# Windowed attention and a split-precision FFN on one core: probabilities moved for two chunks at once, ring loads taken from ScalarE's queue, runs of attention two pairs apart

## The chip, the cores and the metric

The kernel runs on one core of one Trainium2 chip. The metric is the device time of one execution in microseconds. The kernel before took 993.02 us (median of 3 runs, 989.14 to 995.45).

## The reference

```
# q, k, v: (8 batches, 8 heads, 576 tokens, 64), float32
scores = (q @ k^T) / 8;  masked to rel = pos_q - pos_k in [0, 64), else -1e9
p      = exp(scores - rowmax);  p = p / (sum(p) + 1e-9)
x      = (p @ v) laid out as (4608 tokens, 512)
h      = x @ w_in            # 512 -> 2048
g      = h * tanh(softplus(h))
out    = g @ w_out           # 2048 -> 512, float32
```

All of it is float32. The matrix products of the FFN are made of three products of rounded parts (high by high, high by low, low by high).

## The kernel before

**Plain chunks.** The 4608 tokens are 12 chunks of 384. Chunks 0 to 3 are computed in 64 steps n (16 per chunk): a step makes `h_ps` from x and one 128-column slice of `wi` (w_in, resident on chip), ScalarE applies Mish, and the step's `gh`, `gl` go through `wo_h`, `wo_l` into three accumulators `acc`.

**Wides.** The other eight chunks are computed as four "wides" of two chunks. A wide runs through NG=8 "pairs" g, each of two slices of w_in, and a pair is made of seven products (A11, S2, A12, S3, S1, A22, S4, a Strassen-Winograd scheme) in banks `m_ps`, with `u` and `t` as the sums between them. The weights' sums for the seven products are made once (`make_sums`), stored to DRAM in `sums` and streamed back into a ring of two pairs that takes the place of part of `wi` (`load_sums`, called by `next_load` for pair g+2 as soon as the products of pair g have read a piece). The activations' sums are put into other places of `wi` (`SLOTS`) by the `fills`, before the first pair of a wide.

**Attention of a wide.** While a wide is computed, `Wide.run(k)` makes the attention of the next one, a pair of heads k at a time, for both of its chunks ("halves" u). A run first makes the value products of heads k-1 (`at<-pT,v_t`, 24 matmuls per half), then the score products of heads k (`s_ps`). Then DVE masks the scores and finds their maxima, ScalarE takes the exponentials, DVE normalizes (`normal`) and transposes in 32 by 32 blocks into `tr`, and DMAs on SP's queue (`load`, which is `nc.sync`) move the blocks from `tr` to their partitions in `pT` (`each_move`). The value products of a half wait for all moves of that half. `RUNS` says after which pair of the wide before a run stands: `RUNS = {0: 0, 1: 1, 3: 2, 5: 3, 6: 4}`, so run 1 follows one pair after run 0, and run 4 one pair after run 3. The runs of the first wide stand in the last plain steps, at n = 45, 49, 53, 57 and 61 (`first_runs`).

**Shared tiles.** `st0`, `st1` and `st2` are three places of one buffer each. The `tr` of the halves, `w`, `s` and `two` of `make_sums`, and `u` of the wides lie in them in turn, and each new tenant waits until the reads of the last one are over.

**Order.** PE executes in the order in which the code is written. Of the other engines each has its own queue, and its order is set by a scheduler; a queue is worked off strictly in order, and a waiting instruction holds up what is behind it. DMAs take one of eight completion counters in turn (DMAHW0 to DMAHW7 in the rows), and a DMA waits until the one that had its counter before has landed.

Of the kernel before, what the change touches and what calls it, by code (L numbers as in the profile page):

```python
# [10 lines left out]
F32 = mybir.dt.float32  # L11
# [13 lines left out]
TQ = 32  # L25
# [4 lines left out]
def tile_window_attn_mish_ffn(  # L30
# [81 lines left out]
            for k in range(0, TK, TQ):  # L112
                engine.tensor_copy(all_masks[r:r + TQ, :, k:k + TQ], all_masks[r:r + TQ, :, k + TQ:k + 2 * TQ])

    pTs = [const.tile([P, P // 32, HM, 32], F32, name=f"pT{i}") for i in range(2)]
    vec.memset(ident, 0.0)
    masks_built = build_masks(pool, vec)
    both_pT = pTs
    pTs = itertools.cycle(pTs)

    wi = const.tile([P, NF, 2, NC_, P], F32R, name="wi")
# [29 lines left out]
    def at_set(n, name):  # L151
        return ps_at.tile([P, DO], F32, name=name, tag=f"at{n}")
# [615 lines left out]
    atts[3].plan(begin, (starts[3] - ahead - begin) / (NPAIR + 0.5), lag=1.5)  # L768
    begin = starts[3] - ahead

    sums = tc.dram_tile([NG, NPROD, P, 2 * 2 * P], F32, name="sums")
    flat = wi.rearrange("p f l c n -> p (f l c n)")
    RING = NPROD * 2 * 2 * P
    ring = flat[:, :2 * RING].rearrange("p (g m n) -> p g m n", g=2, m=NPROD)
    XS = 2 * 2 * CH
    LOADS = ((0, 2), (2, 4), (4, 6), (6, 7))

    def make_sums(g):

        f0, f1 = 2 * g, 2 * g + 1  # L780
        for m, f, half in ((A11, f0, 0), (A12, f0, 1), (A22, f1, 1)):
            nc.sync.dma_start(sums[g, m].rearrange("p (l n) -> p l n", l=2),
                              wi[:, f, :, 2 * half:2 * half + 2, :].rearrange("p l c n -> p l (c n)").bitcast(F32))
        w = st_home([P, 2, 2, 2 * P], F32, "w", 0)
        parts = [wi[:, f0:f1 + 1, i, :, :].rearrange("p f c n -> p f (c n)").bitcast(F32) for i in range(2)]
        nc.vector.tensor_tensor(w.rearrange("p f h n -> p f (h n)"), *parts, ALU.add)
# [5 lines left out]
        for n, ms in ((2, (S2, S3)), (0, (S1, S4))):  # L792
# [7 lines left out]
    def load_sums(g, first, end):  # L800
# [12 lines left out]
    class Wide:  # L813
# [16 lines left out]
        def run(self, k):  # L830

            at = [at_set(i, "at") for i in range(2)]
            if k >= 1:
                for u, a in enumerate(self.atts):
                    value_products(a.v[k - 1], a.pT.pop(k - 1), [at[u][:, n:n + BLK] for n in range(0, CH, BLK)])
            if k < NPAIR:
                banks = [h_bank("s_ps", DO) for _ in range(2)]
                s_ps = {}
                for u, a in enumerate(self.atts):
                    for m in range(NM):  # L840
                        n = u * NM + m
                        to = [(banks[h], n * TK) if n < 5 else (at[h], CH) for h in range(2)]
                        to = [b[:, i:i + TK] for b, i in to]
                        thin_products(a.qk[k], m, to)
# [12 lines left out]
            units = [new_probs(TK) for _ in range(2)]  # L857
            todo = [(u, h, m) for h in range(2) for u in range(2) for m in range(NM) if (u, m) != (1, NM - 1)]
            todo += [(1, h, NM - 1) for h in range(2)]
            for u, h, m in todo:  # L860
                s = [[None] * NM for _ in range(2)]
                s[h][m] = s_ps[u, h, m]
                done = masked(self.cs[u], units[u], s, [(h, m)])
                if copies and (u, m) == (1, NM - 1):
                    tc.add_manual_dep(done.ins, copies[h].ins.name, SYNC, reason="one reader of a bank at a time")
            for u, a in enumerate(self.atts):
                normal(units[u], BY_HEAD)
                pT, each = run_transpose(units[u][0], both_pT[u], u)
                a.pT[k] = pT, list(each)
                self.after(u, k, "qk")  # L870

        def after(self, u, k, what):
# [31 lines left out]
            yield self.fill(S4, b22)  # L904

        def product(self, g, m, bank, start):
            w = ring[:, g % 2, m, :].rearrange("p (l k n) -> p l k n", l=2, k=2)
# [19 lines left out]
        def pair(self, g, some, between):  # L927
            def bank():
                return h_bank("m_ps")

            def t_tile():
                return mp.tile([P, CH], F32, name="t", tag="t", bufs=TS)

            def add(out_, a, b):
                with tc.high_priority(offset=SOON):
                    nc.vector.tensor_tensor(out_, a, b, ALU.add)  # L936

            u2, u3 = (kept["u"][:, i, :] for i in range(2))
# [7 lines left out]
            self.next_load(g, 0)  # L946
# [6 lines left out]
            self.next_load(g, 1)  # L953
            add(u3, u2, b)
            some(2)
            a = bank()
            self.product(g, S1, a, True)
            t = t_tile()
# [3 lines left out]
            self.next_load(g, 2)  # L962
# [5 lines left out]
            self.next_load(g, 3)  # L968
            t = t_tile()
            add(t, u2, a)  # L970
            units[0, 1] = self.unit(None, t)
            some(2)
            between(g)
            some(NG * NTT)
            return units

        def next_load(self, g, n):
            if g + 2 < NG or self.next:
                load_sums(g + 2, *LOADS[n])
# [87 lines left out]
    for n, (c, f) in enumerate(steps):  # L1067
# [117 lines left out]
```

## Time and profile before

| | |
|---|---|
| median of 3 runs | 993.02 us (989.14 to 995.45) |
| the profiled execution | 991.94 us, span 990.1 us |
| mean granted clock of TensorE in it | 0.952 of full |
| PE busy | 894.3 us, 90% of the span |
| ScalarE (ACT) busy | 459.8 us, 46% |
| VectorE (DVE) busy | 435.0 us, 44% |
| GpSimd (POOL) busy | 240.5 us, 24% |
| queue of DMAs by hardware, q1 | 143.05 MB, 45.4% of 16 engines' time |
| moves of probabilities | 480 of 24 KB, 1.8 us from issue to landing |
| ring loads | 96 of 512 KB and 32 of 256 KB, about 4 us to landing |

Busy time is per engine. PE is busy for nine tenths of the span, so what can be read from the rest is where PE stood still and what released it. The granted clock is the share of full speed (2.4 GHz) that the throttle gave TensorE; 0.5 is its lower level of 1.2 GHz.

### The profile page before, as it was taken

How to read it: one execution, taken by the hardware profiler on the slowest of the kernel's cores; microseconds unless marked ns; L12 is line 12 of the kernel's file. 1: busy time of each engine (PE TensorE's matmuls, PEld its weight loads, DVE VectorE, ACT ScalarE, POOL GpSimd, SP SyncE). 2: the span in 40 equal slices, each digit the busy share in tenths (PEclk: the TensorE clock that was granted, in tenths of full speed). 3: DMA queues.
4: the chain of work that ended last, by engine and by line, in shares of the span. 5: the costliest groups of instructions: out<-in, count | busy, mean ns of one | idle time of the engine just before them, and what ended most of it. 6: DMA issues, size and time to landing. Idle time of an engine off the chain costs nothing.

```text
span 990.1 us, 19444 instructions
## 1 busy us (share of the span) xinstructions
PE 894.3 (90%) x7162; PEld 789.6 (80%) x7162; DVE 435.0 (44%) x1271; ACT 459.8 (46%) x1215; POOL 240.5 (24%) x227
## 2 busy tenths in 40 slices
PE   7899999976886889789979979997989997999998
PEld 5789898865675778678868868886868886998987
DVE  7888886522323123443334532443443441432322
ACT  6757564533535253644354543453543552423222
POOL 4400001432022123212224213133212223422221
PEclk9999999997888898989998989998999997999999
DMA  9665656533344352446435645464553452543401
GB/s 300 217 214 184 205 174 198 174 99 132 97 133 165 96 167 85 131 142 230 157 122 162 203 141 172 126 211 152 173 184 130 153 190 84 160 141 126 117 32 65
DMA packets 127998, 152.09 MB, mean 154 GB/s; under 512 B 14240, under 2 KB 87456, under 8 KB 127904
## 3 DMA queue, kind: packets, MB, share of 16 engines
q1 hardware_dynamic: 122864, 143.05, 45.4%
q10 hardware_dynamic: 5040, 7.80, 2.2%
q8 instruction: 57, 0.93, 0.4%
q14 instruction: 37, 0.30, 0.1%
HBM read 114.88 MB, written 24.12 MB: 140 GB/s over the span
## 4 chain that ended last, share of the span: by engine, by line
PE 51%; SPq 9%; DMA 4%; ACT 2%; DVE 2%; issue 2%; DVEq 0%; ACTq 0%
PE acc L129 25%; PE m_ps L129 20%; SPq L82 9%; PE at L129 3%; PE h_ps L129 2%; ACT pr L82 1%; DMA pT<-tr 1%; PE s_ps L129 1%; DMA v_t<-vN 1%; DMA sums<-two 1%; DVE pr L82 0%; DMA k_t<-kT 0%; ACT L82 0%; DMA wi<-sums 0%; DVE tr L82 0%
## 5 line engine op out<-in xcount | busy, mean ns | idle before, releaser
L129 PE MATMUL acc<-wo_h,gh 128*128 128x512 f32 x576 | 232.1, 408 | 2.8 <-ACT o L383 2.8
L924 POOL TENSOR_TENSOR gl<-t,gh 128x384 fp32r<-128x384 f32 x128 | 134.2, 1050 | 396.7 <-ACT gh L923 134.9
L129 PE MATMUL acc<-wo_l,gh 128*128 128x512 f32 x576 | 229.8, 399 | 0.0
L129 PE MATMUL acc<-wo_h,gl 128*128 128x512 f32 x576 | 226.6, 396 | 0.0
L129 PE MATMUL m_ps<-wi 128*128 128x384 f32 x1152 | 219.1, 337 | 3.7 <-DVE u L936 1.4
L129 PEld LDWEIGHTS m_ps<-wi 128*128 128x128 f32 x1152 | 203.0, 188 | 15.6 <-ACT gh L923 3.0
L129 PE MATMUL h_ps<-xh,wi 128*128 128x384 f32 x512 | 143.7, 343 | 1.9 <-ACT gh L82 1.5
L129 PEld LDWEIGHTS acc<-wo_h,gl 128*128 128x128 f32 x576 | 110.5, 192 | 25.7
L129 PEld LDWEIGHTS acc<-wo_h,gh 128*128 128x128 f32 x576 | 110.8, 193 | 24.3 <-ACT o L383 3.6
L82 ACT ACTIVATE pr<-pr,mx 128x96 f32<-128x96 f32 (+1 forms) x288 | 105.5, 370 | 41.2 <-DVE mx L82 41.1
L129 PEld LDWEIGHTS acc<-wo_l,gh 128*128 128x128 f32 x576 | 111.1, 193 | 15.8
L936 DVE TENSOR_TENSOR u<-u,m_ps 128x384 f32<-128x384 f32 x64 | 35.2, 550 | 162.2 <-PE m_ps L129 162.2
L919 ACT ACTIVATE gh<-t 128x384 fp32r<-128x384 f32 x96 | 50.3, 524 | 116.8 <-DVE t L936 79.6
L129 PEld LDWEIGHTS h_ps<-xh,wi 128*128 128x128 f32 x512 | 95.5, 191 | 5.9 <-ACT gh L82 2.3
L936 DVE TENSOR_TENSOR t<-u,m_ps 128x384 f32<-128x384 f32 x96 | 53.1, 553 | 83.8 <-PE m_ps L129 83.6
L129 PE MATMUL h_ps<-xl,wi 128*128 128x384 f32 x256 | 87.3, 341 | 0.0
L82 DVE CUSTOM_DVE_ANT_0 pr<-s_ps,masks 128x96 f32<-128x96 f32 (+1 forms) x256 | 49.7, 259 | 85.3 <-PE s_ps L129 85.1
L129 PE MATMUL at<-pT,v_t 128*64 128x64 f32 x768 | 33.8, 252 | 55.2 <-DMA pT<-tr 52.8
L129 PEld LDWEIGHTS at<-pT,v_t 128*64 128x64 f32 x768 | 30.1, 163 | 61.9 <-issue 43.3
L82 POOL TENSOR_TENSOR gl<-t,gh 128x384 fp32r<-128x384 f32 x32 | 32.9, 1029 | 113.3 <-ACT gh L82 95.1
L82 ACT ACTIVATE t<-h_ps 128x384 f32<-128x384 f32 x64 | 31.4, 491 | 52.3 <-PE h_ps L129 49.7
L82 ACT ACTIVATION_READ_ACCUMULATOR pr<-pr,mx 128x1 f32 x288 | 54.8, 190 | 0.0
(72 smaller groups left out, 974.3 us busy)
## 6 DMA issues: line engine op xcount, KB each, us to landing
wi<-sums SPq DMA_DIRECT2D x96, 512.0 KB, 3.9
v_t<-vN SPq DMA_DIRECT2D x46, 384.0 KB, 4.8
pT<-tr SPq DMA_DIRECT2D x480, 24.0 KB, 1.8
k_t<-kT SPq DMA_DIRECT2D x44, 224.0 KB, 4.2
q_t<-qT SPq DMA_DIRECT2D x47, 192.0 KB, 4.5
st<-w_in SPq DMA_DIRECT2D x16, 512.0 KB, 4.1
st<-w_out SPq DMA_DIRECT2D x16, 512.0 KB, 4.1
sums<-two SPq DMA_DIRECT2D x32, 256.0 KB, 3.5
```

Source lines behind the costliest of these rows:

```text
L82: i = call(*args, **kw)
L129: i = nc.tensor.matmul(*args, **kw)
L919: nc.scalar.activation(gh, t, AF.Mish)
L924: nc.gpsimd.tensor_tensor(gl, t, gh.bitcast(F32), ALU.subtract)
L936: nc.vector.tensor_tensor(out_, a, b, ALU.add)
```

## The change

Three things change together.

- The probabilities. `pT` of both halves is one tile, and so is `tr` (in st0). A run issues 12 moves of 48 KB (32 partitions of 384 elements, both halves) where it issued 24 of 24 KB, and the values of both halves wait for the same 12.
- The sums. They are stored as one 14 KB line per partition and pair, with 4 stores per pair in place of 7, and made at n = 33, 37, ..., 61, so four of the eight pairs, the fifth to the eighth, are made in the steps in which `first_runs` stand (n = 49, 53, 57 and 61; the fourth at 45). Before, they were made at each odd n from 33 to 47. The ring is loaded by 2 DMAs per pair (1 MB after the product S1, 768 KB after S4) from ScalarE's queue, where it was 4 from SP's queue (after S2, S3, A22 and S4).
- The runs. `RUNS = {0: 1, 2: 2, 4: 3, 6: 4}`, and the last run of a wide, `run(4)`, also scores heads 0 of the wide after. Two runs are always two pairs apart. In the first wide's runs this means that the run at n=61 makes probabilities too.

```diff
-    pTs = [const.tile([P, P // 32, HM, 32], F32, name=f"pT{i}") for i in range(2)]
+    pT_all = const.tile([P, P // 32, 2, HM, 32], F32, name="pT")
+    pTs = [pT_all[:, :, i] for i in range(2)]
...
-    sums = tc.dram_tile([NG, NPROD, P, 2 * 2 * P], F32, name="sums")
+    PIECE = 2 * 2 * P
+    RING = NPROD * PIECE
+    sums = tc.dram_tile([NG, P, RING], F32, name="sums")
...
-    LOADS = ((0, 2), (2, 4), (4, 6), (6, 7))
+    LOADS = (slice(0, 4 * PIECE), slice(4 * PIECE, RING))
...
     def make_sums(g):
...
+        kept_ = [nc.sync.dma_start(sums[g, :, :2 * PIECE], wi[:, f0].rearrange("p l c n -> p (l c n)").bitcast(F32)),
+                 nc.sync.dma_start(sums[g, :, 4 * PIECE:5 * PIECE].rearrange("p (l n) -> p l n", l=2),
+                                   wi[:, f1, :, 2:, :].rearrange("p l c n -> p l (c n)").bitcast(F32))]
         w = st_home([P, 2, 2, 2 * P], F32, "w", 0)
...
+        for i in kept_:
+            tc.add_manual_dep(i.ins, order[-1].name, SYNC, reason="the steps before it first")
...
-            for j, m in enumerate(ms):
-                nc.sync.dma_start(sums[g, m], two[:, j, :, :].rearrange("p l n -> p (l n)").bitcast(F32))
...
+            nc.sync.dma_start(sums[g, :, first * PIECE:(first + 2) * PIECE],
+                              two.rearrange("p m l n -> p (m l n)").bitcast(F32))
+
+    def load_sums(g, part):
         g %= NG
-        nc.sync.dma_start(ring[:, g % 2, first:end, :].bitcast(F32), sums[g, first:end].rearrange("m p n -> p m n"))
+        nc.scalar.dma_start(ring[:, g % 2, part].bitcast(F32), sums[g, :, part])
...
         def run(self, k):
...
+            scored = self if k < NPAIR else self.next
...
-            if k == NPAIR:
-                return
+            if scored:
+                scored.probs(k % NPAIR, s_ps, copies)
+
+        def probs(self, k, s_ps, copies):
...
+            tr = st_home([P, TK // TQ, 2, HM, TQ], F32, "tr", 0)
+            for u in range(2):
+                normal(units[u], BY_HEAD)
+                vec.transpose(tr[:, :, u].rearrange("p k j i -> p j k i"), units[u][0].rearrange("p j (k i) -> p j k i", i=32))
+            moves = []
+            for r in range(0, P, TQ):
+                for i in range(TK // TQ):
+                    at = r % BLK + i * TQ
+                    moves.append(load.dma_start(pT_all[at:at + TQ, r // TQ].rearrange("p u j q -> p (u j q)"),
+                                                tr[r:r + TQ, i].rearrange("p u j q -> p (u j q)")))
             for u, a in enumerate(self.atts):
-                normal(units[u], BY_HEAD)
-                pT, each = run_transpose(units[u][0], both_pT[u], u)
-                a.pT[k] = pT, list(each)
+                a.pT[k] = pT_all[:, :, u], moves
...
-        if n >= starts[2] // 2 and n % 2 and sums_made < NG:
+        if n >= starts[2] // 2 and n % 4 == 1 and sums_made < NG:
             make_sums(sums_made)
...
-    RUNS = {0: 0, 1: 1, 3: 2, 5: 3, 6: 4}
+    RUNS = {0: 1, 2: 2, 4: 3, 6: 4}
```

**SP's queue around a run of a wide.** Before, the moves of the halves (to `pT_78` and `pT_79`) stand between ring loads (`wi<-sums`), with the loads of the next heads' v, q and k behind:

```order
222 L82 DMA k_t<-kT 128x448
223 L802 DMA wi<-sums 128x2x512
224 L82 DMA pT_78<-tr 32x192 x12
225 L82 DMA pT_79<-tr 32x192 x12
226 L802 DMA wi<-sums 128x2x512 x2
227 L802 DMA wi<-sums 128x512
228 L82 DMA v_t<-vN 128x6x128 x2
```

With the change:

```order
157 L82 DMA k_t<-kT 128x448
158 L82 DMA q_t<-qT 128x384
159 L82 DMA k_t<-kT 128x448
160 L82 DMA pT<-tr 32x384 x12
161 L82 DMA v_t<-vN 128x6x128 x2
162 L82 DMA q_t<-qT 128x384
163 L82 DMA k_t<-kT 128x448
```

The queue holds 12 moves in place of 24, each twice as wide, and no ring load.

**DVE where the plain steps end.** Before, the rows from the last normalization of run 3 on: a transpose, the low halves of the fills (`wi<-...`, L884) and the first sums of the first pair (`u`, `t`, L936):

```order
602 L82 TENSOR_TENSOR pr<-pr,sm 128x576 [waits DVE_49]
603 L82 STREAM_TRANSPOSE tr<-pr 128x6x3x32 [waits DMAHW4_49,DMAHW3_49,DMAHW5_49,DMAHW2_49,DMAHW6_49,DMAHW1_49,DMAHW7_49,DMAHW0_49,DVE_49]
604 L884 TENSOR_TENSOR wi<-xn_3907,wi 128x768 [waits PE_49,Activation_49]
605 L884 TENSOR_TENSOR wi<-t_4199,wi 128x768 [waits Activation_49]
606 L884 TENSOR_TENSOR wi<-xn_3354,wi 128x768 [waits PE_49,Activation_49]
607 L884 TENSOR_TENSOR wi<-t_4198,wi 128x768 [waits PE_49]
608 L884 TENSOR_TENSOR wi<-t_4199,wi 128x768 [waits PE_49,Activation_49]
609 L884 TENSOR_TENSOR x_4197<-xn_3907,x_4197 128x768 [waits Activation_49]
610 L936 TENSOR_TENSOR u<-u,m_ps 128x384 [waits PE_49,Activation_49]
611 L936 TENSOR_TENSOR u<-u,m_ps 128x384 [waits DVE_49,PE_49]
```

With the change, the rows from the last fill ahead of the transposes on (the sums of the last pair of weights are `w` and `s`; DMAHW0 to DMAHW7 of the row of `w` are the 12 moves from `tr`, since both lie in st0; the fills are L907 here, and `u`, `t` L959):

```order
630 L907 TENSOR_TENSOR x_4225<-xn_3805,x_4225 128x768 [waits PE_49,Activation_49]
631 L82 STREAM_TRANSPOSE tr<-pr 128x6x3x32 [waits DMAHW2_49,Pool_49]
632 L82 STREAM_TRANSPOSE tr<-pr 128x6x3x32 [waits DVE_49]
633 L796 TENSOR_TENSOR w<-wi 128x1024 [waits DMAHW4_49,DMAHW3_49,DMAHW5_49,DMAHW2_49,DMAHW6_49,DMAHW1_49,DMAHW7_49,DMAHW0_49,DVE_49]
634 L803 TENSOR_TENSOR s<-w 128x256 [waits DVE_49]
635 L803 TENSOR_TENSOR s<-w 128x256
636 L907 TENSOR_TENSOR wi<-t_4226,wi 128x768
637 L803 TENSOR_TENSOR s<-s,w 128x256 [waits DVE_49]
638 L907 TENSOR_TENSOR wi<-t_4227,wi 128x768 [waits Activation_49]
639 L803 TENSOR_TENSOR s<-w,s 128x256 [waits DVE_49]
640 L959 TENSOR_TENSOR u<-u,m_ps 128x384 [waits DMAHW7_49,PE_49,Activation_49]
```

Two transposes of run 4 and the `w` of the eighth `make_sums` now stand here, and `w`, which waits for the moves, is ahead of two of the fills' low halves and of the first `u`.

**ScalarE at the same place, and at a ring load.** Before, the end of the plain steps and the first pair (`u<-m_ps` is the copy of the product A11, L922 and L923 the first quadrant's Mish):

```order
321 L883 CAST wi<-t_4199 128x768 [waits PE_49,Pool_49]
322 L82 ACTIVATE t<-h_ps 128x384 [waits PE_49]
323 L82 ACTIVATE gh<-h_ps 128x384
324 L883 CAST x_4197<-xn_3907 128x768 [waits Activation_49]
325 L943 COPY u<-m_ps 128x384 [waits DMAHW7_49,DMAHW0_49,PE_49]
326 L922 ACTIVATE t<-m_ps 128x384 [waits PE_49]
327 L923 ACTIVATE gh<-m_ps 128x384
```

With the change (L807 rounds the sums to their high parts, L966 is the copy of A11, L945 and L946 the Mish, L942 and L943 that of the next quadrant, L383 and L388 copy and store an output tile):

```order
330 L906 CAST wi<-t_4227 128x768 [waits DMAHW7_49,DVE_49,Pool_49]
331 L807 CAST two<-s 128x2x256 [waits DMAHW1_49,DVE_49,Activation_49]
332 L807 CAST two<-s 128x2x256 [waits DMAHW3_49,DMAHW4_49,DMAHW2_49,DMAHW5_49,DMAHW1_49,DMAHW6_49,DMAHW0_49,DMAHW7_49,DVE_49,Activation_49]
333 L966 COPY u<-m_ps 128x384 [waits DMAHW7_49,PE_49,Pool_49]
334 L945 ACTIVATE t<-m_ps 128x384 [waits PE_49]
335 L946 ACTIVATE gh<-m_ps 128x384
336 L814 DMA wi<-sums 128x2048 [waits PE_49]
337 L383 COPY o<-acc_3368 128x512 [waits PE_49]
338 L388 DMA out<-o 128x512 [waits Activation_49]
339 L942 ACTIVATE gh<-t 128x384 [waits DVE_49]
```

The copy of A11 into `u` has two roundings for `make_sums` ahead of it, and waits for DMAHW7, which is the store of `two` that lies in st2, where `u` will lie. The ring load (L814) stands behind the Mish of the first quadrant and ahead of that of the second.

## Rows read from the trace of the kernel before

**Rows 1.** Page, part 1: busy time, share and instructions of each engine.

```profile
PE 894.3 (90%) x7162; PEld 789.6 (80%) x7162; DVE 435.0 (44%) x1271; ACT 459.8 (46%) x1215; POOL 240.5 (24%) x227
```

**Rows 2.** Page, part 4: the chain of work that ended last, by engine.

```profile
PE 51%; SPq 9%; DMA 4%; ACT 2%; DVE 2%; issue 2%; DVEq 0%; ACTq 0%
```

**Rows 3.** Waits of PE: total us, times, longest.

```profile
PE at L129 <- DMA pT<-tr: 52.8, 10, 6.8
PE o_ps L129 <- DMA pT<-tr: 19.0, 4, 6.2
```

**Rows 4.** Timeline, PE, first wide's runs: start, us, instruction, [idle before <-releaser].

```profile
289.02 1.55 PE L129 MATMUL at<-pT,v_t 128*64 128x64 f32 x24 [4.02 <-DMA pT<-tr]
...
323.29 1.55 PE L129 MATMUL at<-pT,v_t 128*64 128x64 f32 x24 [6.16 <-DMA pT<-tr]
...
347.10 1.62 PE L129 MATMUL at<-pT,v_t 128*64 128x64 f32 x48
...
372.85 1.55 PE L129 MATMUL at<-pT,v_t 128*64 128x64 f32 x24 [5.08 <-DMA pT<-tr]
```

**Rows 5.** Timeline, PE, two runs one pair apart.

```profile
417.35 0.92 PE L129 MATMUL at<-pT,v_t 128*64 128x64 f32 x24 [0.97 <-DMA pT<-tr]
...
424.53 1.55 PE L129 MATMUL at<-pT,v_t 128*64 128x64 f32 x24 [6.26 <-DMA pT<-tr]
...
431.85 1.38 PE L129 MATMUL m_ps<-wi 128*128 128x384 f32 x7
```

**Rows 6.** Timeline, PE, a run two pairs after the last, and the run after it.

```profile
460.57 1.62 PE L129 MATMUL at<-pT,v_t 128*64 128x64 f32 x48
...
466.28 2.25 PE L129 MATMUL m_ps<-wi 128*128 128x384 f32 x12
...
495.00 1.62 PE L129 MATMUL at<-pT,v_t 128*64 128x64 f32 x48
```

**Rows 7.** Windows around them: us, busy of five engines, granted clock, DMA share, GB/s.

```profile
400.00:450.00 50.00, 40.55 (x367) 35.39 (x349) 19.57 (x79) 24.16 (x74) 9.10 (x9) 0.90 0.40 121
450.00:500.00 50.00, 50.00 (x507) 44.44 (x506) 20.10 (x77) 23.59 (x64) 13.94 (x13) 1.00 0.64 211
```

**Rows 8.** Timeline, SP's queue: moves of an attention step, and of a wide run.

```profile
215.12 7.49 SPq L82 DMA_DIRECT2D pT<-tr  x12
...
562.48 16.52 SPq L82 DMA_DIRECT2D pT<-tr  x24
```

**Rows 9.** Timeline, PE: scores of a wide run begin.

```profile
555.54 1.13 PE L129 MATMUL s_ps<-k_t,q_t 64*32 64x96 f32 x76
```

**Rows 10.** Timeline, DVE: second transpose of that run.

```profile
565.10 0.78 DVE L82 STREAM_TRANSPOSE tr<-pr 128x576 f32<-128x576 f32 x1
```

**Rows 11.** Page, part 6: KB each, median us from issue to landing.

```profile
wi<-sums SPq DMA_DIRECT2D x96, 512.0 KB, 3.9
...
pT<-tr SPq DMA_DIRECT2D x480, 24.0 KB, 1.8
...
sums<-two SPq DMA_DIRECT2D x32, 256.0 KB, 3.5
```

**Rows 12.** Timeline, DVE: the w of a pair's sums, and a transpose behind its stores.

```profile
301.33 1.27 DVE L786 TENSOR_TENSOR w<-wi 128x1024 f32<-128x1024 f32 x1 [1.90 <-DMA sums<-two]
...
313.21 0.78 DVE L82 STREAM_TRANSPOSE tr<-pr 128x576 f32<-128x576 f32 x1 [5.38 <-DMA sums<-two]
```

**Rows 13.** Timeline, PE: first and third product of the first pair.

```profile
386.88 2.27 PE L129 MATMUL m_ps<-wi 128*128 128x384 f32 x12
...
393.83 2.27 PE L129 MATMUL m_ps<-wi 128*128 128x384 f32 x12
```

**Rows 14.** Timeline, DVE: a low half of the fills.

```profile
386.64 1.15 DVE L884 TENSOR_TENSOR x<-xn,x 128x768 fp32r<-128x768 f32 x1 [0.59 <-ACT x L883]
```

**Rows 15.** Timeline, ACT's queue: one issue there.

```profile
394.65 0.34 ACTq L388 DMA_DIRECT2D out<-o  x1
```

**Rows 16.** Waits of SP's queue.

```profile
SPq L802 <- PE m_ps L129: 230.5, 77, 14.3
```

More of the change, by code (lines that the diff above doesn't have):

```diff
@@ L769, in tile_window_attn_mish_ffn, with piece, at @@
     begin = starts[3] - ahead
-    sums = tc.dram_tile([NG, NPROD, P, 2 * 2 * P], F32, name="sums")
+    PIECE = 2 * 2 * P
+    RING = NPROD * PIECE
+    sums = tc.dram_tile([NG, P, RING], F32, name="sums")
     flat = wi.rearrange("p f l c n -> p (f l c n)")
-    RING = NPROD * 2 * 2 * P
-    ring = flat[:, :2 * RING].rearrange("p (g m n) -> p g m n", g=2, m=NPROD)
+    ring = flat[:, :2 * RING].rearrange("p (g n) -> p g n", g=2)
     XS = 2 * 2 * CH
-    LOADS = ((0, 2), (2, 4), (4, 6), (6, 7))
+    LOADS = (slice(0, 4 * PIECE), slice(4 * PIECE, RING))
+    def piece(g, m):
+        def at(first, order="p (l k n) -> p l k n"):
+            return ring[:, g % 2, first * PIECE:(first + 1) * PIECE].rearrange(order, l=2, k=2)
+        if m in (A11, A12):
+            both = ring[:, g % 2, :2 * PIECE].rearrange("p (l h k n) -> p l h k n", l=2, h=2, k=2)
+            return both[:, :, m == A12]
+        return at({S2: 2, S3: 3, A22: 4, S1: 5, S4: 6}[m])
     def make_sums(g):
         f0, f1 = 2 * g, 2 * g + 1
-        for m, f, half in ((A11, f0, 0), (A12, f0, 1), (A22, f1, 1)):
-            nc.sync.dma_start(sums[g, m].rearrange("p (l n) -> p l n", l=2),
-                              wi[:, f, :, 2 * half:2 * half + 2, :].rearrange("p l c n -> p l (c n)").bitcast(F32))
+        kept_ = [nc.sync.dma_start(sums[g, :, :2 * PIECE], wi[:, f0].rearrange("p l c n -> p (l c n)").bitcast(F32)),
+                 nc.sync.dma_start(sums[g, :, 4 * PIECE:5 * PIECE].rearrange("p (l n) -> p l n", l=2),
+                                   wi[:, f1, :, 2:, :].rearrange("p l c n -> p l (c n)").bitcast(F32))]
         w = st_home([P, 2, 2, 2 * P], F32, "w", 0)
         parts = [wi[:, f0:f1 + 1, i, :, :].rearrange("p f c n -> p f (c n)").bitcast(F32) for i in range(2)]
-        nc.vector.tensor_tensor(w.rearrange("p f h n -> p f (h n)"), *parts, ALU.add)
+        kept_.append(nc.vector.tensor_tensor(w.rearrange("p f h n -> p f (h n)"), *parts, ALU.add))
+        for i in kept_:
+            tc.add_manual_dep(i.ins, order[-1].name, SYNC, reason="the steps before it first")
         s = st_home([P, 4, 2 * P], F32, "s", 1)
@@ L791, in make_sums @@
             nc.vector.tensor_tensor(out_, a, b, op)
-        for n, ms in ((2, (S2, S3)), (0, (S1, S4))):
+        for n, first in ((2, 2), (0, 5)):
             two = st_home([P, 2, 2, 2 * P], F32R, "two", n)
@@ L796, in make_sums @@
             nc.gpsimd.tensor_tensor(two[:, :, 1, :], s[:, i, :], two[:, :, 0, :].bitcast(F32), ALU.subtract)
-            for j, m in enumerate(ms):
-                nc.sync.dma_start(sums[g, m], two[:, j, :, :].rearrange("p l n -> p (l n)").bitcast(F32))
-    def load_sums(g, first, end):
+            nc.sync.dma_start(sums[g, :, first * PIECE:(first + 2) * PIECE],
+                              two.rearrange("p m l n -> p (m l n)").bitcast(F32))
+    def load_sums(g, part):
         g %= NG
-        nc.sync.dma_start(ring[:, g % 2, first:end, :].bitcast(F32), sums[g, first:end].rearrange("m p n -> p m n"))
+        nc.scalar.dma_start(ring[:, g % 2, part].bitcast(F32), sums[g, :, part])
     SLOTS = [flat[:, 2 * RING + j * XS:2 * RING + (j + 1) * XS] for j in range(NPROD - 1)]
@@ L835, in run @@
                     value_products(a.v[k - 1], a.pT.pop(k - 1), [at[u][:, n:n + BLK] for n in range(0, CH, BLK)])
-            if k < NPAIR:
+            if scored:
                 banks = [h_bank("s_ps", DO) for _ in range(2)]
                 s_ps = {}
-                for u, a in enumerate(self.atts):
+                for u, a in enumerate(scored.atts):
                     for m in range(NM):
@@ L843, in run @@
                         to = [b[:, i:i + TK] for b, i in to]
-                        thin_products(a.qk[k], m, to)
+                        thin_products(a.qk[k % NPAIR], m, to)
                         for h in range(2):
@@ L854, in run @@
                     self.after(u, k - 1, "v")
-            if k == NPAIR:
-                return
+            if scored:
+                scored.probs(k % NPAIR, s_ps, copies)
+        def probs(self, k, s_ps, copies):
             units = [new_probs(TK) for _ in range(2)]
@@ L906, in product @@
         def product(self, g, m, bank, start):
-            w = ring[:, g % 2, m, :].rearrange("p (l k n) -> p l k n", l=2, k=2)
+            w = piece(g, m)
             x = SLOTS[m].rearrange("p (l k n) -> p l k n", l=2, k=2)
@@ L945, in pair @@
             self.product(g, S2, b, True)
-            self.next_load(g, 0)
             add(u2, u3, b)
@@ L952, in pair @@
             self.product(g, S3, b, True)
-            self.next_load(g, 1)
             add(u3, u2, b)
@@ L957, in pair @@
             self.product(g, S1, a, True)
+            self.next_load(g, 0)
             t = t_tile()
@@ L961, in pair @@
             self.product(g, A22, b, False)
-            self.next_load(g, 2)
             t = t_tile()
@@ L967, in pair @@
             self.product(g, S4, a, False)
-            self.next_load(g, 3)
+            self.next_load(g, 1)
             t = t_tile()
@@ L978, in next_load @@
             if g + 2 < NG or self.next:
-                load_sums(g + 2, *LOADS[n])
+                load_sums(g + 2, LOADS[n])
         def out_products(self, g, units, f, t):
@@ L1106, in tile_window_attn_mish_ffn @@
             for part in LOADS:
-                load_sums(f - 7, *part)
+                load_sums(f - 7, part)
     strict[0] = True
```

1 line of the change is left out of this document (removed).

## The prediction

> **What bounds the kernel now.** I read the busy shares first, then what PE waited for, then the stretches in which it waited. PE is busy for 894.3 of 990.1 us [rows 1], and no other engine for half of them, so the time can only come from PE's 95.8 us of idling and from the speed at which its products run. The chain that ended last says the same and names the other party: 51% PE, 9% SP's queue, 4% DMAs [rows 2]. PE's list of waits says what for: ten waits of value products for the moves of probabilities, 52.8 us, and four of the attention of the last plain chunk, 19.0 us [rows 3], together three quarters of the idling. Three of the ten, 4.02 + 6.16 + 5.08 = 15.3 us, lie in the first wide's runs [rows 4]. So seven, 37.5 us, lie in the wides.
>
> Those seven come from runs that follow one pair after another. In such a run [rows 5] the first half's values wait 0.97 us, the second half's 6.26. A run two pairs after the last [rows 6] has its 48 value matmuls in one piece with no wait. Why can be read from SP's queue: the 24 moves of a run take it 16.52 us, the 12 of one chunk 7.49 [rows 8], some 0.6 to 0.7 us each, while scores to the second transpose take 565.88 - 555.54 = 10.3 us [rows 9, 10] and the landing 1.8 [rows 11]. That is 10 + 16 + 2 = 28 us, less the 3 or so by which the first half's moves start before the second transpose, about 25. Two pairs and a run take PE 495.00 - 460.57 = 34.4 us [rows 6], so one pair and a run some 19.
>
> A stall also costs the clock. From the first value product to the next product after the run takes 431.85 - 417.35 = 14.50 us with the stall [rows 5] and 466.28 - 460.57 = 5.71 without [rows 6]. Of the difference of 8.79 us, 6.26 is idling; the other 2.5 are products at the lower level: 24 value matmuls take 1.55 us behind the stall and 0.92 ahead of it [rows 5]. The granted clock of that stretch was 0.90, and 1.00 in the next, where PE never stood still [rows 7]. TensorE's levels are 1.2 and 2.4 GHz, so 0.90 is a fifth of the stretch at the lower.
>
> **The change, part by part.** The sum is made against the profiled execution, 991.9 us, which is 1.1 below the median of the runs.
>
> *Runs two pairs apart, and 12 moves.* Scores to landing become 10.3 + 12 x 0.69 (16.52/24) + 1.8 = 20.4 us, plus about 1 since both transposes come ahead of the first move. From one run to the next PE now always has the 34.4 us of [rows 6]. So the waits in the wides go, with more than 10 us in hand: -37.5 us. They would stay gone if a move of 48 KB took twice the issue time. Six of the seven are long enough to cost clock (the seventh is 0.97): -6 x 2.5 = -15. Bounds: half of that comes back, or all.
>
> *ScalarE's ring loads.* 64 issues there in place of 128 on SP; at 0.34 us [rows 15] that is 22 us of ScalarE's queue, which is busy 46% [rows 1]. The order puts the load behind the first quadrant's Mish, and behind it the Mish of a quadrant whose product comes after the load's release. So the load's own wait on PE holds up nothing: 0. If that cover is gone, each pair slips (a rival below). The loads also share the DMA engines with the moves; a landing that takes 4 us as ring loads do [rows 11], not 1.8, eats 2 of the 10 us in hand: 0.
>
> The row on SP [rows 16] shows 230.5 us in which ring loads waited for PE ahead of whatever stood behind them. The Trainium skill, "DMA: Bandwidth & Descriptors", section "Issuing engines are not separate DMA queues", speaks against a gain from this part: DMAs started by different engines interleave on the same 16 engines, and only issue time is saved. By it this part is worth nothing beyond the queue, and the sum has no term for bandwidth.
>
> *Last plain chunk's attention.* Its moves keep their size and number. Half the sums are made there now, and a pair's sums cost DVE 1.27 us for w [rows 12] and four smaller adds, which stood ahead of some of these chains. Of the 19.0 us I take off 2.5; bounds 0 and -6.
>
> *The first wide's runs.* Here each run now shares st0 with the sums of one pair: `tr`, then `w`, then one `two`, then the next `tr`. The chain without sums is 20.4 us from the start of the scores; PE has four steps and a run, 372.85 - 5.08 - 0.92 - 347.10 = 19.8 between the last two, of which the earlier did not wait [rows 4]. With sums, `w` waits for the moves with the next masks behind it on DVE, and the next transposes wait for the store of `two`: w to that transpose took 313.21 - 301.33 = 11.9 us [rows 12]. That gives waits of 2 to 5 us for each of four runs, 8 to 20 in all, against 15.3 before. I take 10, near the lower end, since the stores overlap with the next scores: -5. Bounds: -15 (all gone) and +12 (each run waits about 7.5).
>
> *Where the plain steps end.* A wait that was not there before. At n=61 run 4 now makes probabilities, and the eighth pair's sums follow in the same tile. On DVE, `w` waits for all 12 moves, with two of the fills' low halves behind it (1.15 us each [rows 14]); ScalarE's roundings wait for `s`; and the copy of A11 into `u` waits for the store of `two` from st2. PE's third product, A12, accumulates where that copy reads. Count from the first value product of run 4. PE's work up to A12 is 0.92 + 393.83 - 372.85 = 21.9 us, less 2.5 of clock, 19.4 [rows 4, 13]. The chain: transposes done by 13 (8 if nothing holds them, 16 if stores and fills do), 12 moves 8.3, landing 1.8, then w to the stores 11.9 and two low halves 2.3, less 1.3 since st2's store is the first: 36. The stall is 16 us, with 2.5 of clock 18.5. Bounds: 10 (nothing holds the transposes, no low halves) and 24. The other engines have nothing late behind it, since DVE and ScalarE catch up while PE has products.
>
> Sum: 991.9 - 37.5 - 15 - 2.5 - 5 + 18.5 = 950.4, and 1.1 for the runs' median: **951 us**.
>
> **The rivals.**
>
> 1. *Forecast*, 0.52: gain in the wides, half of it less a new stall. 938 to 966.
> 2. *The stall at the end of the plain steps is short.* For: DVE's order is the scheduler's, and the stores of two may land early. Against: `w` needs the last move. Without it 951 - 18.5 = 932; with the first runs' waits gone too, 922. 0.18.
> 3. *A move costs by its bytes.* 12 of 48 KB then take 16 us. Against: an issue of 512 KB lands in 3.9 us [rows 11], so bytes are not what an issue of 24 KB pays for. The wides don't mind (28 us of 34.4), but the four first runs wait 8 us more each and the end of the plain steps too: 951 + 40 = 991, within 1% of now. With half of that, 971. 0.15 for the two, a third of it at the full price.
> 4. *ScalarE stands behind its ring loads: slower.* Besides PE, a ring load waits for the DMA that had its counter, often a move of the last run. Then ScalarE's in-order queue holds the Mish and the copy of A11, and PE runs out of banks. Ring loads waited 230.5 / 77 = 3.0 us each on SP [rows 16]; once per pair on 30 pairs that is 90 us: 1041. It decides from (41.5 + 10)/30 = 1.7 us per pair. Against: by position the moves waited for are landed, or land within 2 us. 0.07.
> 5. *The waits only move.* The waits of the wides turn up behind another tile (banks of `at`, v loads) or the clock stays low: 985 to 1000. 0.08.
>
> **How the numbers follow.** The time is the forecast's, 951. The range of 926 to 981 takes in case 2 but for its lowest end, the bounds of the first runs (+17) and the last stall (+5.5), half the clock (+7.5), and leaves out the full price of case 3 and most of 4 and 5. A difference under 1%, 10 us, can't be told from none. Faster by more: all of 1 and 2, most of 3, a little of 5: 0.83. Same: 0.09. Slower: 0.08, case 4 and a little of 5.
>
> **What would show it.** Right: no wait of `at` for moves of over 1 us after the first pair; windows of the wides at clock 0.99 or 1.00; 12 moves in 7.5 to 9 us on SP; a wait of PE of 8 to 20 us, in one or two pieces, around the first A11 and A12, with DVE's `w` behind the last move. Wrong: moves of 1.3 us; waits of m_ps for ScalarE in every pair; waits of 6 us or more in each first run.

## The result, and the profile after

The changed kernel takes 948.61 us (median of 4 runs, 947.39 to 950.41), where the kernel before took 994.24 in the same comparison: a ratio of 0.9549, 95% interval 0.9505 to 0.9592. The forecast was 951, in a range of 926 to 981. The profiled execution has a span of 945.8 us (before 990.1) and a mean granted clock of 0.969 (before 0.952).

The page after, parts 1 and 4 (as in [rows 1, 2]):

```profile
PE 879.3 (93%) x7162; PEld 778.8 (82%) x7162; DVE 440.5 (47%) x1271; ACT 459.8 (49%) x1215; POOL 240.1 (25%) x227
...
PE 55%; DMA 4%; DVE 4%; ACT 3%; issue 2%; SPq 2%; POOL 0%; ACTq 0%; DVEq 0%; POOLq 0%
```

PE is busy 93% of a shorter span, and SP's queue has all but left the chain that ended last: 9% before, 2% now. PE's waits (total us, times, longest):

```profile
PE m_ps L129 <- ACT u L966: 19.7, 2, 18.4
PE o_ps L129 <- DMA pT<-tr: 12.7, 3, 6.0
PE acc L129 <- ACT o L383: 7.1, 1, 7.1
PE at L129 <- DMA pT<-tr: 5.5, 2, 3.0
PE m_ps L129 <- DVE u L959: 3.3, 4, 1.2
PE m_ps L129 <- DVE t L959: 3.0, 2, 1.5
```

The 52.8 us of value products waiting for moves [rows 3] are 5.5, and none of that is in the wides. In their place stands one wait for a copy on ScalarE, 18.4 us. A run of a wide on PE's timeline (start, us, instruction):

```profile
435.83 1.62 PE L129 MATMUL at<-pT,v_t 128*64 128x64 f32 x48
...
441.54 1.73 PE L129 MATMUL m_ps<-wi 128*128 128x384 f32 x9
...
470.26 1.62 PE L129 MATMUL at<-pT,v_t 128*64 128x64 f32 x48
```

No idle time in front of it, 5.71 us to the next product as in [rows 6], and 34.43 us to the next run. The wides as one window, of the kernel after and then of the kernel before (length, busy us of PE, PEld, DVE, ACT, POOL; granted clock, DMA share, GB/s):

```profile
420.00:945.80 525.80, 515.58 (x3878) 457.93 (x3876) 210.39 (x561) 230.58 (x583) 146.85 (x134) 1.00 0.48 154
```

```profile
431.85:990.10 558.25, 521.77 (x3865) 463.43 (x3863) 208.53 (x569) 232.47 (x592) 147.76 (x132) 0.97 0.45 145
```

PE is busy 515.6 of 525.8 us at a clock of 1.00; before it was 521.8 of 558.3 at 0.97. The moves in SP's queue, of run 4 of the first wide and of a run in a wide:

```profile
372.72 7.48 SPq L82 DMA_DIRECT2D pT<-tr  x12
...
447.40 8.22 SPq L82 DMA_DIRECT2D pT<-tr  x12
```

Twelve moves of 48 KB take 7.5 to 8.2 us here and at most 9.2 in the other runs but one (10.9), where twelve of 24 KB took 7.5 [rows 8]. Part 6 of the page:

```profile
wi<-sums ACTq DMA_DIRECT2D x32, 1024.0 KB, 5.2
...
pT<-tr SPq DMA_DIRECT2D x192, 48.0 KB, 3.5
```

A move's landing went from 1.8 to 3.5 us, with a megabyte often in flight beside it. The megabyte alone is not the reason: in experiment 3 it is loaded from SP's queue, and a move of 48 KB lands in 2.0 us. In experiment 7 moves of 24 KB land in 1.9 us, with the loads on ScalarE's queue.

**Where the plain steps end.** PE's timeline from the values of run 4 to the product A12:

```profile
353.98 2.83 PE L129 MATMUL at<-pT,v_t 128*64 128x64 f32 x48 [3.04 <-DMA pT<-tr]
...
368.57 2.27 PE L129 MATMUL m_ps<-wi 128*128 128x384 f32 x12
...
390.60 4.21 PE L129 MATMUL m_ps<-wi 128*128 128x384 f32 x12 [18.38 <-ACT u L966]
```

DVE in the same stretch: the last fill's low half ahead of the transposes, the two transposes, `w`, and the low half behind it:

```profile
368.75 2.59 DVE L907 TENSOR_TENSOR x<-xn,x 128x768 fp32r<-128x768 f32 x1
...
371.26 1.43 DVE L82 STREAM_TRANSPOSE tr<-pr 128x576 f32<-128x576 f32 x2
...
381.73 1.23 DVE L796 TENSOR_TENSOR w<-wi 128x1024 f32<-128x1024 f32 x1 [9.04 <-DMA pT<-tr]
...
383.67 0.95 DVE L907 TENSOR_TENSOR wi<-t,wi 128x768 fp32r<-128x768 f32 x1
```

And ScalarE, the second rounding of the sums and the copy of A11:

```profile
386.24 0.62 ACT L807 CAST two<-s 128x512 fp32r<-128x512 f32 x1 [0.59 <-DVE s L803]
...
390.07 0.48 ACT L966 COPY u<-m_ps 128x384 f32<-128x384 f32 x1 [3.21 <-DMA sums<-two]
```

The transposes end at 372.7, `w` starts at 381.73 when the last move has landed (9.04 us of idle time ahead of it), the roundings follow `s`, and the copy of A11 waits 3.21 us for the store of `two`. PE stands for 18.38 us, and its next twelve matmuls take 4.21 us, at the lower clock, where the same twelve took 2.27 [rows 13].

**By stage.** Cut at the fourth value product of the last plain chunk's attention (262.02, now 252.85), at the first values of run 4 (372.85 - 5.08 - 0.92 = 366.85, now 353.98) and at the product A12 (390.36, now 390.60):

| stage | before | after | difference | forecast |
|---|---|---|---|---|
| up to the last plain chunk's fourth values | 262.0 | 252.9 | -9.2 | -2.5 |
| first wide's runs, to run 4 | 104.8 | 101.1 | -3.7 | -5 |
| run 4 to A12 | 23.5 | 36.6 | +13.1 | +18.5 |
| A12 to the end | 599.7 | 555.2 | -44.5 | -52.5 |
| span | 990.1 | 945.8 | -44.3 | -41.5 |

Two waits stand on other sides of these cuts than in the forecast. Before, run 4's wait of 5.08 us comes behind the second cut, now its 3.04 us ahead of it. With both ahead of it the two middle rows are -8.8 and +18.2. And the slow matmuls behind the new stall are in the row from A12 on: from A12 to the next product it takes 396.92 - 390.60 = 6.32 us now, and 393.83 - 390.36 = 3.47 before. The forecast had 2.5 us for that in the row above. Without these 2.9 us the last row is -47.4.

### The profile page after: what moved, and what is told of

Its sections match the earlier page's. It is cut to its first block, busy times and chain, and to the rows that moved or that the text cites. A ratio compares the mean times of both kernels' runs of the same rounds, so it can differ in the third digit from the quotient of the medians.

```text
span 945.8 us, 18947 instructions
## 1 busy us (share of the span) xinstructions
PE 879.3 (93%) x7162; PEld 778.8 (82%) x7162; DVE 440.5 (47%) x1271; ACT 459.8 (49%) x1215; POOL 240.1 (25%) x227
## 4 chain that ended last, share of the span: by engine, by line
PE 55%; DMA 4%; DVE 4%; ACT 3%; issue 2%; SPq 2%; POOL 0%; ACTq 0%; DVEq 0%; POOLq 0%
PE acc L129 27%; PE m_ps L129 23%; DMA sums<-two 3%; PE at L129 3%; ACT pr L82 2%; DVE wi L907 2%; SPq L82 2%; PE s_ps L129 2%; DMA out<-o 1%; PE h_ps L129 1%; DVE sm L82 1%; DVE pr L82 1%; ACT xn L865 0%; DMA pT<-tr 0%; DVE tr L82 0%
## 5 line engine op out<-in xcount | busy, mean ns | idle before, releaser
L129 PE MATMUL m_ps<-wi 128*128 128x384 f32 x1152 | 221.7, 340 | 24.1 <-ACT u L966 19.7
L129 PEld LDWEIGHTS m_ps<-wi 128*128 128x128 f32 x1152 | 204.2, 189 | 37.3 <-ACT u L966 21.0
L129 PE MATMUL acc<-wo_h,gh 128*128 128x512 f32 x576 | 227.9, 400 | 7.1 <-ACT o L383 7.1
L129 PE MATMUL acc<-wo_l,gh 128*128 128x512 f32 x576 | 226.8, 394 | 0.0
L129 PE MATMUL acc<-wo_h,gl 128*128 128x512 f32 x576 | 224.3, 392 | 0.0
L129 PEld LDWEIGHTS acc<-wo_h,gh 128*128 128x128 f32 x576 | 108.6, 189 | 26.7 <-ACT o L383 7.5
L129 PEld LDWEIGHTS acc<-wo_l,gh 128*128 128x128 f32 x576 | 109.0, 189 | 15.5
L942 ACT ACTIVATE gh<-t 128x384 fp32r<-128x384 f32 x96 | 50.4, 526 | 125.8 <-DVE t L959 84.9
L959 DVE TENSOR_TENSOR u<-u,m_ps 128x384 f32<-128x384 f32 x64 | 35.3, 552 | 140.2 <-PE m_ps L129 135.8
L959 DVE TENSOR_TENSOR t<-u,m_ps 128x384 f32<-128x384 f32 x96 | 53.1, 553 | 84.3 <-PE m_ps L129 84.3
L1032 DVE TENSOR_TENSOR acc_sb<-acc_sb,acc 128x512 f32<-128x512 f32 x56 | 38.4, 686 | 34.8 <-PE acc L129 34.8
L943 ACT ACTIVATE t<-t 128x384 f32<-128x384 f32 x96 | 50.2, 525 | 8.7 <-PE m_ps L129 0.5
```

The costliest lines, as they stand in the source:

```text
L129: i = nc.tensor.matmul(*args, **kw)
L942: nc.scalar.activation(gh, t, AF.Mish)
L943: nc.scalar.activation(t, t, AF.Mish)
L1032: nc.vector.tensor_tensor(total, total, acc, ALU.add)
```

## The experiments

Each kernel is timed against the kernel before on the same chip (990.9 to 991.8 us there, 994.2 with the changed kernel above). Differences of some 5 us between two of these kernels are therefore read from their traces too.

**1. The spacing alone.** The kernel before, with

```diff
+            scored = self if k < NPAIR else self.next
...
-            if k == NPAIR:
-                return
+            if scored:
+                scored.probs(k % NPAIR, s_ps, copies)
...
-    RUNS = {0: 0, 1: 1, 3: 2, 5: 3, 6: 4}
+    RUNS = {0: 1, 2: 2, 4: 3, 6: 4}
```

> The kernel before with one part of the change alone: runs always two pairs apart, with run(4) scoring heads 0 of the wide after. Moves stay 24 of 24 KB, ring loads 4 per pair on SP's queue, sums at each odd n from 33 to 47. Theory (the spacing alone takes the waits out of the wides, and the stall at the end of the plain steps comes from the later sums, which are not here): PE's wait for the moves in the wides falls from 37.5 us to under 2, the clock there is 0.99 or more, there is no stall over 4 us at the first A11 or A12, and the first wide's runs keep their some 15 us; 994 - 37.5 - 9 = about 946 us, 939 to 953. Rival (the fewer moves or the ring's own queue are needed too): waits of 15 us or more stay in the wides, over 965 us.

947.15 us, ratio 0.9542 (0.9501 to 0.9583). PE's waits:

```profile
PE o_ps L129 <- DMA pT<-tr: 18.2, 4, 6.1
PE at L129 <- DMA pT<-tr: 13.8, 3, 6.3
...
PE m_ps L129 <- DVE t L939: 3.0, 2, 1.5
```

The three waits for moves that are left, 13.8 us, are in the first wide's runs. The wides have none, and there is no stall at A12. So this part alone brings what the whole change brings. The other parts, on top of it, come to nothing in the sum: what they gain ahead of the wides the new stall takes back.

**2. The spacing undone** in the changed kernel (`RUNS` as before, `scored = self if k < NPAIR else None`).

> The changed kernel with the runs spaced as before (after pairs 0, 1, 3, 5, 6, run(4) scores nothing); 12 moves of 48 KB, ring loads on ScalarE's queue and the later sums stay. Theory (chain of a run with 12 moves 21 to 23 us against some 18 from one run to the next one pair later): six waits of 3 to 5 us, about 24 us, and some 9 of clock come back in the wides; the stall of 18.4 us at the first A12 goes, since run 4 makes no probabilities there, so the last sums wait for no moves: 948.6 + 33 - 20 = about 962 us, 954 to 970. Rival A (the number of moves is not what set the wait): six waits of 6 us or more, 975 us or more. Rival B (the stall at A12 has another cause): the stall stays, 980 us or more.

973.24 us, ratio 0.9809 (0.9768 to 0.9849). The time is above the theory's range. PE's timeline, at A12 and at one of the runs:

```profile
378.66 4.21 PE L129 MATMUL m_ps<-wi 128*128 128x384 f32 x12 [8.28 <-ACT u L966]
...
506.66 2.83 PE L129 MATMUL at<-pT,v_t 128*64 128x64 f32 x48 [4.45 <-DMA pT<-tr]
```

Six waits of 4.41 to 6.97 us, 30.9 in all where I had 24, stand in the wides (before, the same six made 36.6): fewer moves alone shorten the chain, but not under one pair and a run. The stall at A12 did not go, it fell to 8.28 us. DVE shows why:

```profile
353.57 1.23 DVE L796 TENSOR_TENSOR w<-wi 128x1024 f32<-128x1024 f32 x1 [9.07 <-DMA pT<-tr]
...
366.50 2.56 DVE L907 TENSOR_TENSOR x<-xn,x 128x768 fp32r<-128x768 f32 x1 [2.19 <-ACT x L906]
...
368.99 2.04 DVE L796 TENSOR_TENSOR w<-wi 128x1024 f32<-128x1024 f32 x1
```

The sums of the seventh pair wait 9.07 us for the moves of run 3, and those of the eighth come behind four fills, at 368.99. So it is not run 4's moves alone that made the stall: the last sums of the weights stood there at all, with st0 and st2 taken in turn. Run 4's probabilities, which are left out here with their moves, make a little over half of it.

**3. The ring loads on SP's queue** in the changed kernel.

```diff
-        nc.scalar.dma_start(ring[:, g % 2, part].bitcast(F32), sums[g, :, part])
+        nc.sync.dma_start(ring[:, g % 2, part].bitcast(F32), sums[g, :, part])
```

> The changed kernel with the two ring loads per pair issued from SP's queue, as before, in place of ScalarE's. Theory (the queue of the ring loads is worth nothing once there are 10 us in hand; the load after S1 stands ahead of the 12 moves on SP and holds them by 2 to 4 us): no wait for moves over 1 us in the wides, 948.6 within 4 us either way. Rival (SP's loads that wait for PE hold up moves or the v, q and k loads behind them): waits of 2 us or more per run, over 960 us.

943.07 us, ratio 0.9506 (0.9474 to 0.9537): 5.5 us less than the changed kernel (4.3 by the ratios, 5.9 by the spans of the traces), a little outside the 4 expected. In the wides nothing changed: runs stand 34.5 us apart, and none waits for moves. 3.6 us of the gain are there before A12, and the rest by the second run after it. ScalarE of the changed kernel, in the first wide's runs, and then of this one:

```profile
288.31 1.28 ACT L82 ACT_TABLE_LOAD   x1 [4.37 <-DMA sums<-two]
...
290.37 0.59 ACT L383 COPY o<-acc 128x512 f32<-128x512 f32 x1
```

```profile
285.25 1.28 ACT L82 ACT_TABLE_LOAD   x1 [0.73 <-DMA sums<-two]
...
287.30 0.59 ACT L383 COPY o<-acc 128x512 f32<-128x512 f32 x1
```

In the changed kernel ScalarE's queue stands 4.37 us (here 0.73) until a store of `two` lands. The likely reason is that the output store in front has the counter which that `two` had before it; the rows name the store of `two`, not the counter. ScalarE's copy of an output tile comes 3.1 us later, and PE's next `acc` waits 7.12 us (here 3.48).

**4. The sums made early**, at each odd n from 33 to 47, in the changed kernel.

```diff
-        if n >= starts[2] // 2 and n % 4 == 1 and sums_made < NG:
+        if n >= starts[2] // 2 and n % 2 and sums_made < NG:
```

> The changed kernel with the sums made at each odd n from 33 to 47, as before, and all else changed. Theory (the stall of 18.4 us at the first A12 comes from the eighth pair's sums behind run 4's moves in the same tile): the stall is gone or under 4 us, ScalarE's wait of 7.1 us for an output tile in the first wide's runs goes too, and the attention of the last plain chunk waits 2 to 8 us longer: about 928 us, 920 to 936. Rival (fills or run 4's own probabilities hold the first pair): a stall of 8 us or more stays at the first A11 or A12, 938 us or more.

937.37 us, ratio 0.9448 (0.9407 to 0.9488). The stall at A12 is gone (0.92 us), so the late sums were its cause, with run 4's probabilities (experiment 2) for half of its size; but the time is 1.4 us over the range. The wait of `acc` for an output tile, which I had expected to go, is still 4.30 us. PE's timeline, the last plain chunk's fourth values and run 1's:

```profile
261.07 1.55 PE L129 MATMUL o_ps<-pT,v_t 128*64 128x64 f32 x24 [9.34 <-DMA pT<-tr]
...
320.93 2.83 PE L129 MATMUL at<-pT,v_t 128*64 128x64 f32 x48 [5.93 <-DMA pT<-tr]
```

The first waits 9.34 us, with a `w` of the sums among the steps of its chain on DVE. The second comes from st0. DVE, the `w` of the seventh pair and the transposes of run 1:

```profile
281.17 1.22 DVE L796 TENSOR_TENSOR w<-wi 128x1024 f32<-128x1024 f32 x1 [9.42 <-DMA pT<-tr]
...
308.94 1.44 DVE L82 STREAM_TRANSPOSE tr<-pr 128x576 f32<-128x576 f32 x2 [8.99 <-DMA sums<-two]
```

`w` waits for the moves of run 0, and run 1's transposes wait 8.99 us for the store of the eighth pair's `two`.

**5. Early sums, and ring loads on SP's queue** (the edits of 3 and 4 together).

> The changed kernel with two parts undone, each of which was faster alone: sums at each odd n from 33 to 47, and ring loads on SP's queue. Theory (they act in different places: the sums at the end of the plain steps, the queue in the first wide's runs, where output stores on ScalarE's queue stand behind a DMA counter; in the wides neither counts): the gains add up in part, 937.4 - 3 = about 934 us, 929 to 938; the runs of the wides stand 34.4 to 34.5 us apart, as in both. Rival (the queue's gain came with the later sums and is none without them): 937 to 941 us.

929.51 us, ratio 0.9362 (0.9319 to 0.9405). The gains add up in full, not in part: 7.9 us under experiment 4.

**6. The same with even steps**, n = 32 to 46 (`n % 2 == 0`).

> As the one with the early sums and SP's queue, but the sums at each even n from 32 to 46, one step earlier. Theory (what the early sums cost now is that the last two meet runs 0 and 1 in st0: w waits 9.4 us for the moves of run 0, the transposes of run 1 wait 9.0 for the store of two, and PE 5.9 for the moves; with the eighth sums behind run 0 and none behind run 1 that wait goes): 934 - 6 = about 928 us, 922 to 934; the first wide's runs wait under 3 us. Rival (st0 is taken in turn however the steps stand): 934 us or more.

920.36 us, ratio 0.9278 (0.9244 to 0.9311), below the range expected. PE's waits:

```profile
PE o_ps L129 <- DMA pT<-tr: 16.3, 4, 5.1
PE m_ps L129 <- DVE u L959: 5.2, 5, 1.7
PE acc L129 <- ACT o L383: 3.3, 1, 3.3
```

No wait for moves is left in the wides or the first wide's runs, and no stall over 1.7 us at A12. This is the fastest of all, 28 us under the changed kernel.

**7. Twenty-four moves of 24 KB** in the changed kernel.

```diff
+                    for u in range(2):
+                        moves.append(load.dma_start(pT_all[at:at + TQ, r // TQ, u].rearrange("p j q -> p (j q)"),
+                                                    tr[r:r + TQ, i, u].rearrange("p j q -> p (j q)")))
```

> The changed kernel with 24 moves of 24 KB in place of 12 of 48 KB, from the same tile, the values waiting for all 24. Theory (an issue costs 0.6 to 0.7 us whatever it carries, so a run's chain grows by 8 us: in the wides it stays under the 34.4 us between runs and costs nothing; the first wide's runs and the stall at the first A12 have no slack): no wait for moves over 1 us in the wides, each of four first runs 5 to 9 us more and the stall 26 us in place of 18.4: 948.6 + 38 = about 986 us, 975 to 996. Rival (bytes, not issues, set the time of the moves, or the chain is hidden in the plain steps too): under 960 us.

968.96 us, ratio 0.9761 (0.9725 to 0.9798), below the range expected. SP's queue, and PE at run 3 and at A12:

```profile
356.35 15.74 SPq L82 DMA_DIRECT2D pT<-tr  x24
```

```profile
344.25 2.83 PE L129 MATMUL at<-pT,v_t 128*64 128x64 f32 x48 [7.27 <-DMA pT<-tr]
...
411.82 4.21 PE L129 MATMUL m_ps<-wi 128*128 128x384 f32 x12 [21.15 <-ACT u L967]
```

Twice the issues take twice the time with the same bytes, 15.74 us. The wides don't notice (no wait for moves). Ahead of them runs 1 to 4 wait 5.1 to 7.3 us (the profile names the moves as releaser at runs 3 and 4 only) and the stall grows to 21.15. Both grew by less than the 8 us that I had expected, 20 us in all where I had 38. A move of 24 KB lands 1.6 us sooner than one of 48 KB (1.9 against 3.5), which is part of it; that the rest was hidden behind waits for st0 is not shown.

**8. Even steps alone**, ring loads on ScalarE's queue.

> The changed kernel with the sums made at each even n from 32 to 46 and nothing else: the ring loads stay on ScalarE's queue. Theory (ScalarE's queue costs some 6 us ahead of the wides, as the two comparisons so far gave: 948.6 to 943.1 and 937.4 to 929.5): 920.4 + 6 = about 926 us, 922 to 931, the runs of the wides 34.4 to 34.5 us apart as on SP's queue. Rival (the queue only mattered where sums and runs met): within 2 us of 920.4.

925.77 us, ratio 0.9341 (0.9303 to 0.9378). ScalarE's queue costs 5.4 us here, 7.9 between experiments 4 and 5, and 5.5 in experiment 3. The runs of the wides stand 34.49 us apart with it as without it. `acc` waits 6.87 us for ScalarE's copy, in experiment 6 3.34.

**9. Spacing and even steps** on the kernel before, 24 moves.

> The kernel before with the spacing of the runs and the sums at each even n from 32 to 46; 24 moves of 24 KB, 7 stores and 4 ring loads per pair on SP's queue as before. Theory (in the first wide's runs only the fewer moves take the waits away: scores to landing take 25 us with 24 moves and PE has 19.8): three or four waits of 4 to 6 us stay there, about 942 us, 936 to 950. Rival (the order of the sums took the waits away, the number of moves does not matter): no wait over 2 us in the first wide's runs, under 930 us.

942.09 us, ratio 0.9519 (0.9458 to 0.9581). The time is the one expected; the waits are only partly so. In the first wide's runs 3.04 and 3.18 us stand at moves, smaller than the 4 to 6 expected, and the last plain chunk's attention waits 21.4 us where it waited 16.3 in experiment 6. Against experiment 6 the 12 moves, the fewer stores and loads and the line of 14 KB are worth 22 us together, all ahead of the wides' steady part; this run does not split them. In the changed kernel, with its later sums, the moves alone are worth 20 us (experiment 7).

## Why the prediction was right

**The wides: right, with one size too large.** All seven waits went (-37.5). The clock was booked at 2.5 us for each of six stalls. I had taken that from [rows 5], the dearest of those that also make scores. A stalled run of the kernel before, later on:

```profile
580.29 1.55 PE L129 MATMUL at<-pT,v_t 128*64 128x64 f32 x24 [6.54 <-DMA pT<-tr]
...
586.64 2.27 PE L129 MATMUL m_ps<-wi 128*128 128x384 f32 x12
```

From the second half's values to the next product it takes 6.35 us, the run of [rows 5] 7.32, and the run of [rows 6] 466.28 - 460.57 - 1.62/2 = 4.90. So this stall cost 1.45 us of clock, where I had 2.5. And the wides got small waits that I had at nothing, at 1.00 of the clock: DVE's sums come late where run 4 of a wide now makes probabilities shortly before the fills. (They come with the spacing: experiment 1 has all six, experiment 2 one.)

```profile
519.54 1.32 PE L129 MATMUL m_ps<-wi 128*128 128x384 f32 x6 [0.59 <-DVE u L959]
...
523.74 1.32 PE L129 MATMUL m_ps<-x,wi 128*128 128x384 f32 x6 [1.49 <-DVE t L959]
...
553.31 1.32 PE L129 MATMUL m_ps<-wi 128*128 128x384 f32 x6 [0.87 <-DVE u L959]
```

There are six such, 6.3 us in all, where three took 1.4 before, which is 4.9 us against. The wides as a whole, from the product behind A12 to the end, before and after:

```profile
393.83:990.10 596.27, 549.90 (x4207) 487.46 (x4205) 222.85 (x636) 252.84 (x652) 154.81 (x139) 0.96 0.46 147
```

```profile
396.92:945.80 548.88, 536.34 (x4111) 476.38 (x4109) 222.40 (x604) 245.73 (x626) 152.18 (x139) 1.00 0.50 157
```

They are 47.4 us shorter, where I had 52.5. PE is busy 13.6 us less. Of that 1.3 is a block of 96 score matmuls which run 4 of the first wide now makes ahead of A12, and which the sum had no term for. That leaves some 12 us for the clock, 2.0 per stall, in place of 15.

**ScalarE's ring loads at nothing: right in the wides, wrong ahead of them.** By experiments 3, 5 and 8 the queue costs 5 to 8 us, nearly all of it before the wides' steady part. Rival 4 had the kind of wait, ScalarE's queue held up by another queue's DMA, but at the wrong place and in the wrong instruction: not the ring load in each pair, but the output stores among the plain steps. That a DMA counter is what ties them is argued, as said in experiment 3.

**The rule of the Trainium skill** ("DMA: Bandwidth & Descriptors", "Issuing engines are not separate DMA queues"), that a second issuing engine saves only issue time, agrees with these runs as far as they go: in the wides the queue is worth nothing, the runs stand 34.4 to 34.5 us apart with either.

**The last plain chunk's attention: mis-sized.** -9.2 us, outside its bound of -6. The waits fell from 19.0 to 12.7 us, where experiments 1 and 4, with all eight sums there, have 18.2 and 18.4. So half the sums were worth 6 us of waits. Of the other 2.9 us, 1.1 was there ahead of these waits already, and 1.0 is PE's work between them, the same 364 matmuls at a granted clock of 0.90 in place of 0.86 (busy 37.3 us, before 38.4). The last 0.8 is open.

**The first wide's runs: right in sign, the waits too large.** I had waits at each of four runs, 8 to 20 us in all, and took 10. Two of the four waited, 2.46 and 3.04 us, 5.5 in all. Against that a wait that the sum had no term for, of `acc` for ScalarE's output copy, grew from 2.8 to 7.12 us. Cut behind the waits of run 4 the stage is -8.8, where I had -5. (The upper bound of +12 also stands for waits of 6.8 us each, not of 7.5.)

**The stall where the plain steps end: mechanism right, the size right by luck.** From run 4's values to the copy I had 36 us; to A12 behind the copy it took 390.60 - 353.98 = 36.6. But the pieces are others. The transposes were done 18.7 us after the first value product, where I had 13, and 16 at the most: the fills' low halves ahead of them took up to 2.59 us each, not 1.15. The moves with their landing took 9.0 us where I had 10.1, and from `w` to A12 it was 8.9 where I had 12.9. And the row at 393.83 that [rows 13] name the third product is not A12. A product has six matmuls, a row of twelve is two products, and A12 begins at 390.36. PE's work up to it is 3.5 us less than I counted, 15.9, so the sum should have had a stall of 20 us. The work took 36.62 - 18.38 = 18.2 us, 2.3 more, since run 4's values waited for moves after all and ran at the lower clock (48 in 2.83 us, in a wide 1.62); so the stall was 18.4. The errors partly cancelled. Experiment 2 adds that the stall would be half as long without run 4's probabilities, whose moves the prediction had as its whole cause.

**The sum** came out 3 us off because the terms erred both ways: 8 us too much from A12 on, 11 too little ahead of it. The direction and the range are earned, since experiments 1 and 2 show the spacing to be what took the waits away; that the time came within 3 us is luck. The prediction booked the spacing and the 12 moves as one term, and in the wides experiment 1 needs only the spacing. Of the rivals, 2 fell with the stall of 18.4 us, and 3 fell: 12 moves take 7.5 to 9.2 us, once 10.9, with twice the bytes, and experiment 7 shows the issue's price from the other side. Rival 5, other tiles in place of the old waits, is there to 5 us.

## What to carry to other kernels

When a chain of 25 us meets a consumer that comes back after 19, first ask whether the consumer can come back later: here that alone was worth the whole gain, and it cost no work. Work that is spread out to be out of the way is to be followed to its last piece: the eighth sums met the first user of their place and took back 18 us, and one step's shift of all eight was worth 9. A number of a sum is taken from several stalls, not from the dearest, and a row's name from its count.

## What was not expected of the hardware

- A move's price in the queue is its issue and not its bytes: 24 of 24 KB took 15.08 to 17.25 us in the kernel before, 12 of 48 KB 7.48 to 9.24 in the changed one (once 10.90), so 0.62 to 0.77 us each. The ring load of 1 MB was issued in 0.33; why a small move takes longer is open.
- After 18.38 us of idling twelve matmuls took 4.21 us at the lower clock, against 2.27; after a stall of 6 us the loss was 1.45 to 2.5 us.
- In the first wide's runs the store of `two` held up ScalarE's queue for 4.37 us with the ring loads on that queue, and for 0.73 with them on SP's. Whether the load slowed the store or only the turn of the counters changed is open.
- A move of 48 KB landed in 3.5 us with the ring loads on ScalarE's queue, and in 2.0 with the same loads on SP's, the queue of the moves (experiments 3, 5 and 6). Why is open.
